# A new slot rule for VectorE, and a rearranged end, in a fused attention and MLP kernel

## The chip, the cores and the metric

One core of one Trainium2 chip. The time is device microseconds of one execution, the median of several runs on the same chip; the runs of one kernel lie within about half a microsecond of each other, in the first round up to 1.1 us. Profile spans are about 1.8 us shorter than times; positions count from a span's start.

## The reference, cut to what matters

```python
xn = layernorm(x)                                  # x: 2048 x 512, bfloat16
q = xn @ wq        # 32 heads of 16;  k, v = xn @ wk, xn @ wv: one head, shared
p = softmax(q k^T / 4);  o = p @ v                 # 2048 x 2048 scores for each head
s = o @ wo
g = silu(silu(xn @ w1) @ w2)                       # 512 -> 1792 -> 512
out = x + s * g
```

## The kernel before

The kernel holds its own scheduler. While the program is built, a planner places work on five engines with estimated durations and emits the instructions in that order; nothing is decided on the chip. Changed rules or seeds therefore give another fixed order.

Scores come as 2048 tiles of 128 keys by 512 queries: 32 groups of 64. A tile's exponential is made in one of two ways. **ScalarE** reads one to three tiles from PSUM, and each gives TensorE one PV product. **VectorE** makes an integer from the score with one multiply-add, whose bits read as bfloat16 approximate the exponential; GpSimd adds three constants to the bits of four such tiles at once (three "shifts"), and the tile gives four weighted PV products. A VectorE tile thus spares ScalarE 0.43 us and costs TensorE three more products. Seven PSUM banks hold scores and other products; the eighth collects PV.

The rule that decides how many of the 3 or 4 free banks of a score phase go to VectorE:

```python
bl = dve_backlog(); ab = act_need() - t
...
else:                                               # 3 or 4 banks are free
    want = 2 if n == 4 or ab > a_low else 1         # a_low: 1000 ns, varied at random
    ...
want = min(want, 2 if bl < two else 1 if bl < one else 0)
```

A group takes no new VectorE batch when few of its tiles are left:

```python
while g < NG and nleft[g] < (MARGIN if g < NG - 1 else MARGIN_END):   # 16, and 28 in the last group
    g += 1
```

The end. When the last PV product is placed, `last_norm` normalises on VectorE, each step for both column halves before the next step; then come four row tiles of the output product, four evictions, sums and stores:

```python
for h in range(2): t1.append(... transpose(f_sb[:, k, cols], bank(OB)[:, cols]))
for h in range(2): t2.append(... reciprocal ...)           # waits for t1[1]
for h in range(2): t3.append(... multiply ...)             # waits for t2[1]
for h in range(2): last_on.append(... transpose ...)       # waits for t3[1]
...
# per row tile r: four products o = 0..3 into bank r, those with o < 3 first
stt[r] = pl.add(scaled(tt, r))      # VectorE: fin = bank * 0.25 * tmp (tmp: this row tile's g)
# r < 3: TensorE adds x to fin by identity products, ScalarE copies it out; r = 3: VectorE adds x
...
if st["assigned"] == NG * SLOTS and st["expn"] == len(units) and not tail["made"]:
    make_tail()
```

The softmax here doesn't subtract the row's maximum and nothing guards it: scores larger than these inputs give would overflow.

## Time and profile before

| | before |
|---|---|
| time, median | 672.18 us |
| span of the profile | 670.4 us |
| TensorE / ScalarE / VectorE / GpSimd busy | 98 / 97 / 91 / 85% |
| last exponential on ScalarE ends | 661.5 us |
| last shift on GpSimd ends | 659.0 us |
| last PV product starts | 661.6 us |
| last copy of the output ends | 667.95 us |

A line of the groups or the timeline reads: start and duration (timeline), line, engine, operation, what is written from what is read, shapes and count; in brackets the idle time before it and what ended it. In a timeline line, a count merges instructions of one kind that follow each other. Line numbers belong to each kernel; L1228 before is L1282 after (PV), L860 is L866 (scores), L1157 is L1202 (shifts on GpSimd). The lines themselves are shown in the prediction.

Waits of TensorE are not read from its busy share here but worked out: score phases and runs of column-tiled products have fixed lengths when nothing holds them (the prediction derives them), and what the start-to-start times exceed these by is called "TensorE's waits" below.

### The profile page before, as it was taken

The page shows a single profiled execution, that of the slowest core. Times are in us where ns is not written, and L with a number is a line of the kernel's source. Part 1 is how long each engine was busy: PE and PEld are TensorE (multiplying, and loading weights), DVE is VectorE, ACT ScalarE, POOL GpSimd, SP SyncE. Part 2 cuts the span into 40 slices and gives each one's busy share as a digit, 9 for nine tenths or more (in the row PEclk, how much of TensorE's full clock was granted, in tenths as well). Part 3 has the DMA queues.
Part 4 walks back from the last instruction along what each step waited for, and adds up shares of the span by engine and source line. Part 5 has one row for each costly group of instructions (what it writes and reads, how often), then busy time and mean ns, then how long its engine had stood idle before and what let it go on. Part 6 is the DMA issues. An engine that isn't in the chain of part 4 may idle for free.

```text
span 670.4 us, 21190 instructions
## 1 busy us (share of the span) xinstructions
PE 658.4 (98%) x8958; PEld 191.4 (29%) x8958; DVE 608.6 (91%) x1085; ACT 651.5 (97%) x756; POOL 566.7 (85%) x564
## 2 busy tenths in 40 slices
PE   7999999999999999999999999999999999999997
PEld 4422222222222222222222222222222222222223
DVE  8989999999999999999899999998979999999963
ACT  6999999999999999999999999999999999999995
POOL 3049899998998889989899988898989998889993
PEclk9999999999999999999999999999999999999999
DMA  9500000000000000000000010000000000100000
GB/s 299 165 9 2 2 2 2 2 3 2 2 1 18 18 18 17 2 2 2 2 2 2 2 33 18 18 2 1 2 2 2 2 2 17 34 18 2 2 2 32
DMA packets 11821, 12.86 MB, mean 19 GB/s; under 512 B 1808, under 2 KB 11216, under 8 KB 11728
## 3 DMA queue, kind: packets, MB, share of 16 engines
q1 hardware_dynamic: 10928, 10.78, 5.0%
q8 instruction: 72, 1.18, 0.7%
q10 hardware_dynamic: 800, 0.72, 0.3%
q14 instruction: 21, 0.17, 0.1%
HBM read 8.95 MB, written 2.10 MB: 16 GB/s over the span
## 4 chain that ended last, share of the span: by engine, by line
PE 78%; ACT 12%; DVE 8%; issue 1%; DMA 0%; ACTq 0%; DVEq 0%
PE ps L1228 34%; PE ps L860 26%; PE ps L505 18%; ACT pa_sb L1572 11%; DVE db_sb L1090 3%; DVE stats_sb L452 1%; ACT t_sb L652 1%; DVE u_sb L654 1%; DMA ds_sb<-in_A_x_dram 0%; DVE xnT_sb L532 0%; DVE xn_sb L481 0%; DVE fin_sb L712 0%; DVE f_sb L1275 0%; DVE mv_sb L456 0%; DVE kt_sb L561 0%
## 5 line engine op out<-in xcount | busy, mean ns | idle before, releaser
L1157 POOL INT64_ADD ds_sb<-db_sb x552 | 561.0, 1038 | 87.5 <-DVE db_sb L1090 33.2
L1572 ACT ACTIVATE pa_sb<-ps 128x1024 bf16<-128x1024 f32 (+2 forms) x667 | 619.0, 1040 | 6.4 <-PE ps L860 3.5
L1090 DVE TENSOR_SCALAR db_sb<-ps 128x512 uint16<-128x512 f32 x736 | 474.4, 682 | 38.8 <-PE ps L860 27.5
L1228 PE MATMUL ps<-ds_sb,v_sb 128*32 128x512 bf16 x2208 | 265.9, 383 | 0.0
L860 PE MATMUL ps<-qt_sb,kt_sb 32*128 32x512 bf16 x2048 | 251.8, 385 | 4.4 <-ACT pa_sb L1572 1.1
L1228 PE MATMUL ps<-pa_sb,v_sb 128*32 128x512 bf16 x1312 | 242.4, 383 | 0.0
L1228 PE MATMUL ps<-db_sb,v_sb 128*32 128x512 bf16 x736 | 165.0, 384 | 0.3 <-DVE f_sb L1275 0.3
L860 PEld LDWEIGHTS ps<-qt_sb,kt_sb 32*128 32x128 bf16 x2048 | 63.1, 91 | 277.6 <-ACT pa_sb L1572 149.8
L1228 PEld LDWEIGHTS ps<-ds_sb,v_sb 128*32 128x32 bf16 x2208 | 65.6, 95 | 62.8 <-issue 46.1
L505 PE MATMUL ps<-xnT_sb,w_sb 128*32 128x512 bf16 x896 | 73.2, 384 | 0.0
L1228 PEld LDWEIGHTS ps<-pa_sb,v_sb 128*32 128x32 bf16 x1312 | 59.6, 95 | 36.5 <-issue 24.9
L505 PE MATMUL ps<-w_sb,u_sb 128*32 128x512 bf16 x816 | 64.2, 384 | 0.0
L1228 PEld LDWEIGHTS ps<-db_sb,v_sb 128*32 128x32 bf16 x736 | 40.9, 95 | 21.5 <-issue 14.5
L652 ACT ACTIVATE t_sb<-ps 128x512 bf16<-128x512 f32 x72 | 45.1, 627 | 0.0
L654 DVE SCALAR_TENSOR_TENSOR u_sb<-t_sb,ps 128x512 bf16<-128x512 bf16 x56 | 38.3, 683 | 1.3 <-ACT t_sb L652 0.3
L694 PE MATMUL ps<-w_sb,u_sb 32*128 32x512 bf16 x80 | 30.8, 385 | 0.0
L505 PEld LDWEIGHTS ps<-xnT_sb,w_sb 128*32 128x32 bf16 x896 | 17.5, 94 | 26.6 <-issue 20.6
L654 DVE SCALAR_TENSOR_TENSOR tmp_sb<-t_sb,ps 128x512 bf16<-128x512 bf16 x16 | 11.0, 688 | 12.3 <-ACT t_sb L652 12.2
L505 PEld LDWEIGHTS ps<-w_sb,u_sb 128*32 128x32 bf16 x816 | 15.6, 95 | 22.3 <-issue 18.5
L1275 DVE STREAM_TRANSPOSE f_sb<-ps 128x512 f32<-128x512 f32 x31 | 21.9, 707 | 0.1
L505 PE MATMUL ps<-wo_sb,on_sb 128*32 128x512 bf16 x256 | 19.2, 383 | 0.0
L505 PE MATMUL ps<-xnT_sb,wq_sb 128*32 128x512 bf16 x240 | 18.9, 384 | 0.0
(71 smaller groups left out, 161.9 us busy)
## 6 DMA issues: line engine op xcount, KB each, us to landing
w_sb<-in_B_w_dram SPq DMA_DIRECT2D x2, 1792.0 KB, 13.4
xr_sb<-in_A_x_dram SPq DMA_DIRECT2D x16, 128.0 KB, 2.3
out_dram<-ob_sb SPq DMA_DIRECT2D x16, 128.0 KB, 1.7
ds_sb<-in_A_x_dram SPq DMA_DIRECT2D x3, 512.0 KB, 6.9
wq_sb<-in_A_wq_dram SPq DMA_DIRECT2D x1, 512.0 KB, 5.1
wo_sb<-in_A_wo_dram SPq DMA_DIRECT2D x1, 512.0 KB, 16.0
kt_sb<-kt_sb ACTq DMA_DIRECT2D x4, 112.0 KB, 4.2
ds_sb<-in_A_x_dram ACTq DMA_DIRECT2D x2, 128.0 KB, 2.9
```

Of the source, the lines that this page charges most:

```text
L452: ts_ = pl.add(Task(DV, 593.0, lambda v, t=t: v.bn_stats(stats_sb[:, t, :], x_tile(t)), [xkey(t)], [("st", t)], 1 + j, gate=(lambda j=j: S ...
L505: last = h.matmul(bank(b)[32 * j:32 * (j + 1), 0:n], lhsT=lhs(j), rhs=rhs, start=start, stop=stop, tile_position=(0, 32 * j), skip_group_c ...
L652: t1 = Task(AC, 490.0, lambda a: a.activation(t_sb[:, k, :], src, ACT.Tanh, scale=scale), [held], [("t", k)], 0, [t0])
L654: t2 = Task(DV, T_P, lambda v: v.scalar_tensor_tensor(out=dst, in0=t_sb[:, k, :], scalar=1.0, in1=src, op0=ALU.add, op1=ALU.mult), [held, ...
L694: return (lambda pe: pe.matmul(bank(b), lhsT=u_sb[rows, ft, r * P:(r + 1) * P], rhs=w2_sb[rows, ft, :], start=False, stop=last, tile_posit ...
L860: return pe.matmul(bank(b), lhsT=kt_sb[32 * i:32 * i + 32, g % 2, kt * P:(kt + 1) * P], rhs=qt_sb[32 * i:32 * i + 32, (g // 2) % NQR, :], ...
L1090: bt.P[i] = pl.add(Task(DV, T_P, lambda v, b=b, i=i, bb=bt.b: v.tensor_scalar(db_sb[:, bb, i * NQ:(i + 1) * NQ], bank(b), 128.0 * LOG2E, 1 ...
L1157: whole["po"].append(pl.add(Task(PO, T_P64, lambda g, cols=cols: g.int64_add(ds_sb[:, s, cols].bitcast(U64), db_sb[:, bt.b, cols].bitcast( ...
L1228: h = pe.matmul(bank(OB)[32 * i:32 * (i + 1), :], lhsT=lhs, rhs=rhs, start=s0, stop=s1, tile_position=(0, 32 * i), skip_group_check=True)
L1275: t1 = pl.add(Task(DV, T_TR, lambda v: v.transpose(f_sb[:, k, :], bank(OB)), [("ps", OB)], [("F", k)], 1, [norm.get(("m", g - 2))]))
L1572: op = pl.place(AC, 0.8333 * NQ * n + T_AF, lambda a: a.activation(pa_sb[:, s * NQ:(s + n) * NQ].rearrange("p (b n) -> p b n", n=NQ), ps3[ ...
```

## The change

It keeps the amount of work and moves its order. The slot rule looks at the PV queue: with three free banks VectorE gets two when fewer than about ten PV entries are queued, else one. (For four free banks the new code also has a branch that gives one instead of two.) Ten seeds with a spread of 0.3 replace eight with 0.1. In the last group VectorE may start batches until 20 tiles are left, and may make shifts itself. ScalarE's last tiles (up to six) are done in two query halves, so that the first half is normalised while the second is still being computed. Two of the four last evictions go through ScalarE, the tail's banks are taken in the order in which they come free, and the tail is made as soon as the MLP is finished, before the last exponentials.

```diff
-SEEDS, STRETCH, SPREAD = (1020, 3123, 1104, 3421, 7220, 2660, 1802, 97), 64, 0.1
+SEEDS, STRETCH, SPREAD = (2502, 4652, 1398, 4134, 3319, 6151, 8548, 1413, 942, 5642), 64, 0.3
-MARGIN, MARGIN_END = 16, 28
+MARGIN, MARGIN_END = 16, 20
+Q3, Q4, J3, J4, N3, N4, SOLO = 10, -1, 1, 2, 1, 2, 0          # and QUEUE = 10
+END_DV = 40
+RH, EVR, SC_PRIO, MT_EARLY = 6, (0, 2), 0, 1
 ...
-                want = 2 if n == 4 or ab > a_low else 1
+                queue = sum(len(q) for g in range(st["gO"], min(st["gO"] + 2, NG)) for q in pvq[g])
+                held = any(not a.fixed for a in active)
+                if held:
+                    want = J4 + (queue < vary(Q4)) if n == 4 else J3 + (queue < vary(Q3))
+                else:
+                    want = N4 if n == 4 else max(N3, 2 * (queue < vary(QUEUE)))
+                if ab > a_low:
+                    want = 2
 ...
-                on_place=placed_dv, ports=2, gate=lambda: URG_SPLIT and urgent() or len(shifts) >= DV_MIN))
+                on_place=placed_dv, ports=2, gate=lambda: len(shifts) >= DV_MIN or bt.g == NG - 1 and nleft[bt.g] < END_DV))
 ...
+            if r in EVR:       # in scaled(): ScalarE takes the row tile out of PSUM, VectorE multiplies in SBUF
+                ev = pl.add(Task(AC, 490.0, lambda a: a.activation(xn_sb[:, r, :], bank(b), ACT.Copy, scale=0.25), ...
 ...
-            if st["assigned"] == NG * SLOTS and st["expn"] == len(units) and not tail["made"]:
+            if st["assigned"] == NG * SLOTS and (MT_EARLY and not active and st["job"] == len(jobs) or st["expn"] == len(units)) and not tail["made"] and all(
+                    tt in tmp_task for tt in range(NT - 4, NT)):
 ...
+        def begin_halves():    # the last <= RH tiles of ScalarE, each exponential for columns 0:256, then 256:512
 ...                             # last_norm(g, h) then runs for each half when its own PV products are placed
```

Other new code (wider pieces, a meter for jobs, late or single tiles) is off at these settings: PIECE_MIN of 9 is over the length of the jobs it now names, METER is empty, LATE and SOLO are 0.

## The prediction

> **What bounds the kernel now.** I read the page first (busy shares, the chain), then the groups by form, then TensorE's timeline in mid-kernel, then the waits, and last the timelines of the final 25 us. First the page's first lines and the by-engine line of the chain that ended last:
>
> ```profile
> span 670.4 us, 21190 instructions
> PE 658.4 (98%) x8958; PEld 191.4 (29%) x8958; DVE 608.6 (91%) x1085; ACT 651.5 (97%) x756; POOL 566.7 (85%) x564
> ...
> PE 78%; ACT 12%; DVE 8%; issue 1%; DMA 0%; ACTq 0%; DVEq 0%
> ```
>
> TensorE and ScalarE both look full, but "busy" for TensorE is modelled, so it alone decides nothing. TensorE's own timeline at 302 us shows the structure:
>
> ```profile
> 302.18 0.39 PE L860 MATMUL ps<-qt_sb,kt_sb 32*128 32x512 bf16 x3
> 302.51 0.40 PE L1228 MATMUL ps<-pa_sb,v_sb 128*32 128x512 bf16 x3
> ...
> 303.27 0.39 PE L860 MATMUL ps<-qt_sb,kt_sb 32*128 32x512 bf16 x4
> ...
> 304.14 0.39 PE L860 MATMUL ps<-qt_sb,kt_sb 32*128 32x512 bf16 x3
> ```
>
> Score products (row-tiled, 3 or 4 side by side) alternate with runs of column-tiled products: PV, projections, MLP. Going by starts: a score phase takes 0.32 us (302.18 to 302.51), whether it holds 3 or 4 products; the 12-product run after it 0.76 (302.51 to 303.27); an 8-product run 0.54. So a run costs about 0.216 per four products plus 0.114 for the switch, a score phase 0.321. The kernel before issues 642 score phases and 639 such runs with 1634 rounds of four: 642 x 0.321 + 639 x 0.114 + 1634 x 0.216 = 631.9 us. From the first run to the last the same pieces take 11.6 us more, summed start to start over the whole trace. That 11.6 is all that TensorE ever waits in them; it is spread evenly, 0.4 to 1.1 us per 50 us after the first 100.
>
> ScalarE, starts again: 667 exponentials, 1312 score tiles; a pair (128x1024) goes every 0.90 us, a single every 0.48, so 0.427 per tile plus 0.05 per instruction. With 72 tanh at 0.48: 594 + 34 = 628 us, first exponential at 11.5, last ended at 661.5. It has some 20 us of slack, part of it the prologue. So TensorE is the tighter one; ScalarE stops it for moments only, and they are seldom seen as waits:
>
> ```profile
> ACT pa_sb L1572 <- PE ps L860: 3.5, 10, 1.1
> ```
>
> That is the longest of ScalarE's waits for the exponentials (us in total, times, longest). Last the end: VectorE, then ScalarE, from 646 us on:
>
> ```profile
> 646.61 1.37 DVE L1090 TENSOR_SCALAR db_sb<-ps 128x512 uint16<-128x512 f32 x2
> 650.29 0.69 DVE L654 SCALAR_TENSOR_TENSOR tmp_sb<-t_sb,ps 128x512 bf16<-128x512 bf16 x1 [2.30 <-ACT t_sb L652]
> 660.63 0.69 DVE L654 SCALAR_TENSOR_TENSOR tmp_sb<-t_sb,ps 128x512 bf16<-128x512 bf16 x1 [9.65 <-ACT t_sb L652]
> 662.00 0.78 DVE L1243 STREAM_TRANSPOSE f_sb<-ps 128x256 f32<-128x256 f32 x2 [0.69 <-PE ps L1228]
> 662.70 0.31 DVE L1247 RECIPROCAL rcp_sb<-f_sb 128x8 f32<-128x8 f32 x2
> 662.94 0.46 DVE L1251 TENSOR_TENSOR otr_sb<-f_sb,rcp_sb 128x128 bf16<-128x128 f32 x2
> 663.31 0.76 DVE L1258 STREAM_TRANSPOSE on_sb<-otr_sb 128x256 bf16<-128x256 bf16 x2
> 664.26 2.61 DVE L712 SCALAR_TENSOR_TENSOR fin_sb<-ps,tmp_sb 128x512 bf16<-128x512 f32 x4 [0.18 <-PE ps L505]
> ```
>
> ```profile
> 660.37 1.14 ACT L1572 ACTIVATE pa_sb<-ps 128x1024 bf16<-128x1024 f32 x1
> 665.86 0.60 ACT L1440 ACTIVATE ob_sb<-ps 128x512 bf16<-128x512 f32 x1 [4.35 <-PE ps L1435]
> 666.75 1.20 ACT L1440 ACTIVATE ob_sb<-ps 128x512 bf16<-128x512 f32 x2 [0.30 <-PE ps L1435]
> ```
>
> VectorE makes its last score tile at 647.3 and then is idle for two long stretches, while ScalarE does the rest alone. After the last exponential (661.51) nothing overlaps: PV, both halves of the normalisation on VectorE (2.07 us), four evictions on VectorE (2.61), a sum, a copy, a store. From the last PV product (661.56) to the end of the last copy (667.95) is 6.39 us, and 2.4 more to the end of the span.
>
> **What the Trainium skill says.** "Perfetto Trace Analysis", section Identifying the Most-Contended Engine, says that matmul occupancy is no good measure of how near TensorE is to its limit, because pipelined instructions look smaller. Here it misleads the other way as well (busy hides the switches), so I use start-to-start times. The same page, section Optimizing Scalar/DVE Operations, gives ScalarE on PSUM some 51 ns of overhead per instruction; the trace agrees (0.904 for 1024 columns against 0.477 for 512 leaves 0.05). It also says that where an engine causes bubbles elsewhere, breaking up instructions may let work complete sooner: that is the idea of the halves. "VectorE: DVE Perf Modes", section The perf-mode tier table, lists tensor_scalar in bf16 within SBUF as 4x, 693 ns at 2048 elements; the shifts now also given to VectorE are of this kind (16 bits). No run so far shows one: VectorE has none in the kernel before. GpSimd takes 1.01 us, start to start, for each of its own. "DMA: Bandwidth & Descriptors" has about 2.0 us of fixed cost per transfer; the last store here takes 1.7, and neither kernel can shorten it.
>
> **The change part by part.** I counted instructions in the order in which both builds issue them; no time comes from there.
>
> Total work. Score tiles stay 2048 and VectorE's share stays 736 exactly; so do the 2208 shifted and 736 unshifted PV products. ScalarE keeps 1312 tiles, in 677 instead of 667 instructions (pairs 637 to 624, singles 26 to 41, triples 4 to 6, and 6 half-width ones): +10 x 0.05 = +0.5 us on ScalarE, which has slack. TensorE: score phases 642 to 640, column-tiled runs 639 to 638, rounds 1634 in both: 631.1 against 631.9, so -0.8 us.
>
> The PV-queue rule and the new seeds and spread. They change only who takes which tile and in which order. The rule gives VectorE two of three tiles when the PV queue is short, which turns pairs into singles; the counts (+15 singles) say that it fires rarely. It can only recover part of TensorE's 11.6 us. About 4 us of them lie before 100 us, where the prologue is the cause, so some 7 are in reach. The order was evidently searched again over ten stretches instead of eight; I allow -2.2 us, three tenths of what is in reach, and this is the softest term.
>
> The end margin (28 to 20) and shifts on VectorE (8 of them, GpSimd 552 to 544). VectorE works where it idled 10 us, but its total is unchanged, so it does eight tiles fewer elsewhere. Since TensorE is full in both places, I count 0 for itself. The eight shifts cost about 8 x 0.6 = 5 us of VectorE time (estimate from the skill's figure), inside that idle stretch, and keep GpSimd's queue (back to back from 646.79 to 658.98) from becoming the end when VectorE passes its last tile later.
>
> The halves. The order shows five tiles, not six, in halves: six exponentials in place of three, +3 x 0.05 on ScalarE. The first half's normalisation now runs while ScalarE computes the second half. After the last PV there is one chain: transpose 0.43, reciprocal 0.18, multiply 0.27, transpose 0.42 = 1.30, with waits between perhaps 1.45, instead of 2.07: -0.6.
>
> The evictions. Of the four serial ones (2.61), two go to ScalarE (0.60 each, parallel) and leave a 0.41 multiply, 0.33 start to start, on VectorE. VectorE then has 0.6 + 0.33 + 0.6 + 0.33 + a 0.33 add = 2.2 to its end instead of 2.94, and its first one need not wait for TensorE: the first half's products are done by then. Last copy, counted from the last PV start: 0.4 to the transpose, 1.45, products and evacuation up to 2.9, multiply 3.75, sum 4.2, copy 4.8; before 6.39: -1.6 for halves and evictions together. Against it, 36 output products instead of 52 are left after the last PV, so 16 (four rounds, 0.86 us) move ahead of it. As TensorE is full there, +0.9. Bank choice by release removes waits of at most tenths; counted in these sums.
>
> Sum: -0.8 + 0.9 - 1.6 - 2.2 = -3.7. 672.1 - 3.7 = 668.4 us.
>
> **The rivals.** (1) The search finds nothing and only the end counts: -1.5, so 670.6. For it: TensorE already waits only 1.8% of its time, evenly. (2) The rule really feeds TensorE and most of the reachable 7 us goes: 663 to 665. For it: ScalarE has 20 us of slack, so bubbles come from order alone; against it: counts hardly move. (3) The end is given back: eight later VectorE tiles each bring four PV products that depend on shifts; if they land after the last exponential, or a shift holds the port against GpSimd, TensorE sits idle at about 660 and the time is 671 to 673. The 8 shifts on VectorE speak against it.
>
> **Range and chances.** Between rivals 1 and 2: 665.6 to 670.6 should hold it 8 times in 10. Faster by 2% needs under 658.7: more than all waits of TensorE plus the tail's gain could give; 0.02. Slower by 2% needs +13 us: 0.01. Within 2%: 0.97.
>
> **What would show it.** Right: last PV to last copy about 4.8 us; TensorE's waits, start to start, 9 to 10 us; 8 VectorE shifts of about 0.7 us between the last VectorE score tiles and the last normalisation; ScalarE evacuations beside VectorE's. Wrong: waits unchanged or larger, an idle gap of TensorE before the last PV, or a tail that still takes 6 us.

## The result, and the profile after

The changed kernel takes 669.78 us (669.76 to 669.82, 4 runs), the kernel before 672.18 us beside it: a ratio of 0.9964, interval 0.9947 to 0.9981, so 2.4 us. By the 2% measure it is the same time. It lies in the range predicted, 1.4 us above the value.

The page's span, busy shares, and the chain by engine, after:

```profile
span 668.0 us, 21223 instructions
PE 658.0 (99%) x8962; PEld 191.2 (29%) x8963; DVE 615.0 (92%) x1093; ACT 652.1 (98%) x768; POOL 558.7 (84%) x556
...
PE 74%; ACT 17%; DVE 7%; issue 1%; DMA 0%; POOL 0%; ACTq 0%; DVEq 0%
```

The busy times hardly differ (TensorE 658.4 to 658.0 us). The chain by engine has lost some TensorE and gained ScalarE, but these are shares of the whole span and say nothing of the end: asked for the stretch from 640 us on alone, the chain of either kernel holds no exponential of ScalarE. VectorE's last stretch:

```profile
645.60 3.10 DVE L1196 TENSOR_SCALAR ds_sb<-db_sb 128x2048 uint16<-128x2048 uint16 x5
...
654.35 1.29 DVE L1002 TENSOR_SCALAR db_sb<-ps 128x512 uint16<-128x512 f32 x2 [0.61 <-PE ps L866]
655.67 1.90 DVE L1196 TENSOR_SCALAR ds_sb<-db_sb 128x2048 uint16<-128x2048 uint16 x3
659.28 0.45 DVE L1306 STREAM_TRANSPOSE f_sb<-ps 128x256 f32<-128x256 f32 x1 [1.71 <-PE ps L1282]
...
660.69 0.41 DVE L1306 STREAM_TRANSPOSE f_sb<-ps 128x256 f32<-128x256 f32 x1
...
662.10 0.69 DVE L719 SCALAR_TENSOR_TENSOR fin_sb<-ps,tmp_sb 128x512 bf16<-128x512 f32 x1
...
664.07 0.42 DVE L731 TENSOR_TENSOR ob_sb<-fin_sb,xr_sb 128x512 bf16<-128x512 bf16 x1
```

VectorE makes score tiles until 655.6 us instead of 648.0, and eight shifts at 0.60 us start to start, five of them before its last score tiles and three after. While it made the five, GpSimd stood idle, and went on when they were done (whether for a buffer, or because a shift held the port as the prediction's third rival feared, the trace does not say):

```profile
648.79 1.04 POOL L1202 INT64_ADD ds_sb<-db_sb  x1 [3.60 <-DVE ds_sb L1196]
```

The first half's transpose starts at 659.28, before the last exponential ends. From there VectorE works to 664.49 with hardly a gap, and the chain that ended last runs through it (view --critical: start, us, what):

```profile
659.18 0.07 PE ps L1282
659.25 0.02 issue
659.28 0.46 DVE f_sb L1306
...
660.77 0.34 DVE f_sb L1306
...
662.14 0.65 DVE fin_sb L719
```

So in the changed kernel it is PV of the first half on TensorE, then both normalisations and the evictions on VectorE, that set the end. ScalarE's last stretch:

```profile
657.52 2.64 ACT L1667 ACTIVATE pa_sb<-ps 128x512 bf16<-128x512 f32 x6
661.88 0.60 ACT L714 ACTIVATE xn_sb<-ps 128x512 bf16<-128x512 f32 x1 [1.73 <-PE ps L511]
...
663.72 1.57 ACT L1508 ACTIVATE ob_sb<-ps 128x512 bf16<-128x512 f32 x3 [0.36 <-PE ps L1503]
```

The six half-width exponentials end at 660.16 (1.35 us earlier than the last one before); the last PV product starts at 660.28 (1.29 earlier); the last copy ends at 665.30 instead of 667.95. From last PV to last copy it is 5.02 us instead of 6.38. Of those 2.65 us, 0.3 are lost behind them: from the last copy to the end of the span it takes 2.72 us instead of 2.46. The four stores, before and after, are

```profile
666.48 2.07 SPq L718 DMA_DIRECT2D out_dram<-ob_sb  x4
664.35 1.81 SPq L725 DMA_DIRECT2D out_dram<-ob_sb  x4
```

SyncE issues them one after the other. In the changed kernel the issues follow each other after 0.39, 0.48 and 0.50 us, so the last one comes 0.41 us after the last copy, not 0.14; from issue to landing it takes 1.85 us, as before (1.86). That is the 0.3.

TensorE's waits fall from 11.6 to 9.8 us. But the scores do not come earlier for it: the 1984th score product (the end of the last group but one) starts at 636.5 us before and at 636.3 after. What TensorE has gained by then is in other work. At 636.4 us, 112 MLP products of the second layer (two row tiles) were still to be issued before, and 56 (one row tile) after; VectorE evicts the last row tile's result (its `tmp`) at 660.6 us before, at 651.1 after. Against the 56 stand 12 PV products that are done later (4060 by then instead of 4072). The net 44 are eleven rounds of four, 2.4 us at the prediction's 0.216: about what the smaller waits and the fewer phases make together.

### The profile page after: what moved, and what is told of

The parts are those of the page before. It is cut to its first block, busy times and chain, and to the rows that moved or that the text cites. A ratio compares the mean times of both kernels' runs of the same rounds, so it can differ in the third digit from the quotient of the medians. Undisturbed runs are those within 1.5% of the kernel's fastest.

```text
span 668.0 us, 21223 instructions
## 1 busy us (share of the span) xinstructions
PE 658.0 (99%) x8962; PEld 191.2 (29%) x8963; DVE 615.0 (92%) x1093; ACT 652.1 (98%) x768; POOL 558.7 (84%) x556
## 4 chain that ended last, share of the span: by engine, by line
PE 74%; ACT 17%; DVE 7%; issue 1%; DMA 0%; POOL 0%; ACTq 0%; DVEq 0%
PE ps L1282 32%; PE ps L866 25%; PE ps L511 16%; ACT pa_sb L1717 16%; DVE db_sb L1002 2%; ACT t_sb L669 1%; DVE stats_sb L458 1%; DVE u_sb L671 1%; DVE xnT_sb L538 0%; DMA ds_sb<-in_A_x_dram 0%; DVE xn_sb L487 0%; POOL ds_sb L1202 0%; DVE fin_sb L719 0%; DVE f_sb L1338 0%; DVE mv_sb L462 0%
## 5 line engine op out<-in xcount | busy, mean ns | idle before, releaser
L1202 POOL INT64_ADD ds_sb<-db_sb x544 | 553.1, 1038 | 91.6 <-DVE db_sb L1002 34.9
L1282 PE MATMUL ps<-ds_sb,v_sb 128*32 128x512 bf16 x2208 | 274.4, 383 | 0.0
L1282 PE MATMUL ps<-pa_sb,v_sb 128*32 128x512 bf16 x1317 | 245.8, 382 | 0.0
L1282 PE MATMUL ps<-db_sb,v_sb 128*32 128x512 bf16 x736 | 176.2, 383 | 0.0
L1282 PEld LDWEIGHTS ps<-ds_sb,v_sb 128*32 128x32 bf16 x2208 | 68.4, 95 | 60.4 <-issue 41.9
L1282 PEld LDWEIGHTS ps<-db_sb,v_sb 128*32 128x32 bf16 x736 | 43.7, 95 | 20.3 <-issue 15.6
L618 PE MATMUL ps<-w_sb,u_sb 32*128 32x512 bf16 x76 | 29.2, 384 | 0.0
L1342 DVE TENSOR_TENSOR otr_sb<-f_sb,rcp_sb 128x256 bf16<-128x256 f32 x31 | 12.9, 417 | 1.4 <-POOL ds_sb L1202 1.1
```

The lines of the kernel that those rows point to most:

```text
L618: return (lambda pe: pe.matmul(bank(b), lhsT=lhs(k, rows, 0, P), rhs=rhs(k, rows), start=False, stop=last, tile_position=(32 * i, 0), skip ...
L1202: whole["po"].append(pl.add(Task(PO, T_P64, lambda g, cols=cols: g.int64_add(ds_sb[:, s, cols].bitcast(U64), db_sb[:, bt.b, cols].bitcast( ...
L1282: h = pe.matmul(bank(OB)[32 * i:32 * (i + 1), cols], lhsT=lhs, rhs=rhs, start=s0, stop=s1, tile_position=(0, 32 * i), skip_group_check=True)
L1342: t3 = pl.add(Task(DV, 332.0, lambda v: v.tensor_tensor(o3[:, :, val:val + DH], f3[:, :, val:val + DH], rcp_sb[:, k, :].unsqueeze(2).to_br ...
```

## The experiments

All twelve are versions of the changed kernel, all gave correct results. This table has what their traces show (us); the median of the kernel before beside each was 672.12 to 672.18.

| run | TensorE's waits | last MLP result evicted | last exponential ends | last GpSimd shift ends | last PV starts | last PV to last copy | time |
|---|---|---|---|---|---|---|---|
| before | 11.6 | 660.6 | 661.5 | 659.0 | 661.6 | 6.38 | 672.1 |
| after | 9.8 | 651.1 | 660.2 | 655.1 | 660.3 | 5.02 | 669.8 |
| end alone | 11.9 | 663.0 | 659.5 | 660.5 | 662.3 | 6.56 | 673.3 |
| order alone | 10.8 | 652.3 | 659.7 | 659.3 | 659.7 | 6.71 | 670.8 |
| old rule, new seeds | 12.5 | 663.7 | 659.7 | 661.1 | 662.3 | 6.96 | 673.7 |
| new rule, old seeds | 9.9 | 649.1 | 660.6 | 654.9 | 661.1 | 5.18 | 670.9 |
| new rule, no random numbers | 11.0 | 650.5 | 661.5 | 661.6 | 663.0 | 5.15 | 672.6 |
| old rule, no random numbers | 11.6 | 662.2 | 660.3 | 656.6 | 661.4 | 6.55 | 672.3 |

### The end alone, and the order alone

Edit for the end alone: old rule and old seeds in the changed kernel (with a guard that the tail is made only when all banks are accounted for, since the build failed without it). TensorE's order is that of the kernel before up to its last 85 rows of merged instructions.

```diff
-SEEDS, STRETCH, SPREAD = (2502, ..., 5642), 64, 0.3
+SEEDS, STRETCH, SPREAD = (1020, ..., 97), 64, 0.1
-                (the new rule)
+                want = 2 if n == 4 or ab > a_low else 1
```

> The end's parts alone (halves, evacuations on ScalarE, tail banks, shifts on VectorE, margin 20) with the slot rule and the seeds of the kernel before: TensorE's order is that of the kernel before up to its last 85 rows. Theory A (the order in the middle brought most of it, since the shorter chain after the last PV is paid for by output products that move ahead of it): 671.5 to 672.2 us. Theory B (the end brought its 1.4 us in full and the middle the rest): 670.6 to 671.0 us.

Edit for the order alone, in which TensorE's order is that of the changed kernel up to its last 84 rows:

```diff
-MARGIN_END = 20;  END_DV = 40;  RH, EVR, SC_PRIO, MT_EARLY = 6, (0, 2), 0, 1
+MARGIN_END = 28;  END_DV = 0;   RH, EVR, SC_PRIO, MT_EARLY = 0, (), 0, 0
```

> The slot rule and the seeds alone, the end as in the kernel before: TensorE's order is that of the changed kernel up to its last 84 rows. Theory A: 669.8 to 670.4 us. Theory B: 670.9 to 671.4 us. If the parts add, the savings of this run and of the run with the end alone sum to 2.4 us within 0.4.

Measured: the end alone 673.28 us, ratio 1.0017 (1.0003 to 1.0031), slower than before; the order alone 670.78, ratio 0.9980. Both theories fall in their common assumption that the parts add: -1.1 (slower) and +1.4 us of savings make 0.2, and together they save 2.4. The end costs 1.1 us on the old order and gains 1.0 on the new one. The trace of the end alone says why (TensorE, then ScalarE, then GpSimd):

```profile
661.54 0.83 PE L618 MATMUL ps<-w_sb,u_sb 32*128 32x512 bf16 x2
662.30 0.29 PE L1277 MATMUL ps<-pa_sb,v_sb 128*32 128x256 bf16 x2
662.31 3.73 PE L511 MATMUL ps<-wo_sb,on_sb 128*32 128x512 bf16 x64
```

```profile
658.03 1.42 ACT L1662 ACTIVATE pa_sb<-ps 128x256 bf16<-128x256 f32 x4
662.41 0.60 ACT L669 ACTIVATE t_sb<-ps 128x512 bf16<-128x512 f32 x1 [2.95 <-PE ps L618]
```

```profile
647.33 13.20 POOL L1197 INT64_ADD ds_sb<-db_sb  x13 [2.91 <-DVE ds_sb L1191]
```

ScalarE is done with its exponentials at 659.45, two microseconds before the kernel before, and then waits 2.95 us for TensorE. TensorE is still on PV and on the last MLP row tile (L618 is a piece of it); GpSimd, with thirteen shifts in a row to 660.53, is close behind. The tail may only be made when the MLP is finished, so all 64 output products stand after the last PV, where the changed kernel has 33. In this order TensorE bounds the end. Relieving ScalarE gains nothing, and the four VectorE tiles more that this build has (740 instead of 736) cost TensorE twelve products, some 0.65 us at 0.216 per four.

In the order alone the last PV even starts 0.54 us earlier than in the changed kernel, but the old tail takes 6.71 us after it, 60 output products among them. Against it the changed end is 1.7 us shorter after the last PV and starts 0.54 later: the two terms that the prediction set at -1.6 and +0.9.

### Rule and seeds

The edits are the two halves of the diff of the end alone, each by itself (the old rule also has the guard on the tail); all of the changed end stays.

> The changed kernel with the old rule for VectorE's slots and the new seeds and spread. If the rule is what cuts TensorE's waits (start to start) from 11.6 to 9.8 us, they go back to 11 to 12 us and the time to 671.3 to 672. If the new seeds do it, waits stay at 9.5 to 10.3 us and the time at 669.6 to 670.4.

> The changed kernel with the new rule but the seeds, stretch count and spread of the kernel before. If the rule brings it: 669.6 to 670.4 us, waits below 10.3 us. If the search over seeds brings it: 671 to 672 us, waits 11 us or more.

Measured: old rule with new seeds 673.72 us, ratio 1.0027 (1.0014 to 1.0039); new rule with old seeds 670.87, ratio 0.9981. So the theory of the rule fits better, though both times lie outside what it stated: taking the rule away costs 3.9 us, not 2, and the seeds still bring 1.1. The waits went the way of the rule's theory (12.5, above the 11 to 12 stated, and 9.9). But some of the 3.9 us is the draw: the build with the old rule has two stalls of TensorE, 0.62 us at 408.7 and 0.47 us at 427.7, where the changed kernel has none over 0.15 us between 100 and 650 us. Two draws prove little, so I took a third, without random numbers (both builds also have the guard; built again, the new-rule program is the same without it, as the changed kernel is with it):

```diff
-SEEDS, STRETCH, SPREAD = (2502, ..., 5642), 64, 0.3
+SEEDS, STRETCH, SPREAD = (), 64, 0.0
```

> The changed kernel with no random numbers in its scheduler at all, new slot rule: a third draw of the order. If the rule itself (VectorE gets two of three tiles when fewer than ten PV entries are queued) is what lets TensorE run ahead with the MLP products, 56 of them (one product of the last four) are left at the end of the last-but-one group, as in the changed kernel, and the time is 669.5 to 671.5 us. If the order is luck, it may fall anywhere from 669 to 674.

> The same without random numbers, old slot rule, all the rest of the end as changed. Rule theory: two MLP products (112) are left as in the kernel before, the last tanh comes after the last exponential, and the time is 672.5 to 674.5 us, at least 2 us over the run with the new rule. Luck theory: within 1.5 us of that run, either way.

Measured: 672.60 us with the new rule, 672.28 with the old (the edges of their intervals, 0.9994 and 1.0024, 0.9986 and 1.0019, overlap). The rule as such is therefore not worth 2 us: over three draws it is -2.4, -3.9 and +0.3. Of the first expectation the count of MLP products held and the time did not; the times of the two fit the second expectation's theory of luck. In all three draws the new rule has the last MLP result out by 649 to 652 us, the old one at 662 to 664; and with the old rule, the time from last PV to last copy is 6.5 to 7.0, with the new one 5.0 to 5.2. (All three builds with the old rule have 740 VectorE tiles, those with the new one 736; I did not separate this.)

What takes the gain away in the third draw is in part that it was never there: by 636.4 us the build with the new rule is 56 MLP products ahead of the one with the old rule, but 44 PV products and six score products behind it (in the two other draws at most four and two behind), and TensorE has stalled for 0.56 us at 429.3. At the end GpSimd adds to it:

```profile
651.46 10.16 POOL L1202 INT64_ADD ds_sb<-db_sb  x10 [1.12 <-PE ps L1282]
```

These ten shifts end at 661.62; VectorE made only two in this order. The two halves share a PSUM bank, so the second half's PV may start only when the first half, shifted products and all, has been transposed out of it: the last PV starts at 663.04, 1.6 us after the last exponential.

How can a rule about VectorE's slots make the MLP finish earlier? The kernels, built again with the planner's decisions printed, say that it hardly acts. In the changed kernel it wants another number of tiles than the old rule in 7 of 640 score phases, all before 38 us; in six of them VectorE takes no tile under either rule, so a single decision changes: at 37.2 us of the planner's time VectorE gets two of three tiles and not one. The branch for four banks never changes anything. The builds without random numbers prove it: with that one decision forced, the old rule gives the program of the new rule, instruction for instruction. The traces agree. In each of the three pairs ScalarE's instructions are the same up to the 48th, at 38.4 to 38.6 us, which is a single tile with the new rule and a pair with the old. So the experiments compare two courses of the planner that part at one tile (with seeds the new rule also draws more random numbers, which is a second difference), not feeding by a short PV queue against none; and the three draws are not independent, since ScalarE's order with the new rule is the same in all three up to 273 us. Why the one course has the MLP done earlier stays open.

### The parts of the end, one at a time

On the changed order the parts of the end can be undone singly; the order stays the same up to the last rows.

Without the halves:

```diff
-RH, EVR, SC_PRIO, MT_EARLY = 6, (0, 2), 0, 1
+RH, EVR, SC_PRIO, MT_EARLY = 0, (0, 2), 0, 1
```

> The changed kernel without the two query halves; all else and TensorE's order up to its last ten rows stay. If the halves take the first normalisation out of the last chain as the prediction says (2.07 us on VectorE back in place of 1.41), +0.5 to +1.0 us: 670.3 to 670.8. If VectorE's evictions bound the end whatever the halves, within 0.2 of 669.8.

670.44 us (ratio 0.9975 to before): the halves are worth 0.7 us, inside the first expectation. From last PV to last copy it is 6.09 instead of 5.02, and the last PV starts 0.3 earlier, as fewer output products stand ahead of it (40 after it instead of 33).

All evictions on VectorE:

```diff
-RH, EVR, SC_PRIO, MT_EARLY = 6, (0, 2), 0, 1
+RH, EVR, SC_PRIO, MT_EARLY = 6, (), 0, 1
```

> The changed kernel with all four last evictions on VectorE. VectorE is busy without a gap from 659.3 to 664.5 us in the changed kernel, so two multiplies from PSUM (0.60 each) in place of two from SBUF (0.33) should cost 0.4 to 0.6 us: 670.2 to 670.4. If TensorE's sums or the stores bound the end, within 0.15 of 669.8.

670.01 us (ratio 0.9968): worth 0.2, between the two expectations, and less than VectorE's own saving. VectorE's four evictions take 2.44 us in one run; the last copy ends 0.2 us later after the last PV (5.21 instead of 5.02).

No shifts on VectorE:

```diff
-END_DV = 40
+END_DV = 0
```

> The changed kernel without shifts on VectorE, so eight more on GpSimd. If GpSimd's shifts become the end (the prediction's third rival), GpSimd runs without gaps to about 659 to 661 us, the last PV waits for it and the time is 670.5 to 672. If PV has enough other work, within 0.3 of 669.8.

670.46 us (ratio 0.9974): worth 0.7. Here is GpSimd:

```profile
647.31 12.19 POOL L1202 INT64_ADD ds_sb<-db_sb  x12 [1.00 <-DVE otr_sb L1342]
```

It runs without a gap to 659.50, as long as before the change (658.98), and the last PV starts at 661.02 instead of 660.28, 0.9 us after the last exponential. The theory that GpSimd becomes the end fits, though the time lies just under what it stated (670.5).

The old end margin:

```diff
-MARGIN, MARGIN_END = 16, 20
+MARGIN, MARGIN_END = 16, 28
```

> The changed kernel with the old end margin of 28, so VectorE's last score tiles come earlier. The prediction counted 0 for the margin by itself: within 0.3 of 669.8. If it matters that ScalarE works alone for longer at the end, the last exponential ends about 1 us later and the time is 670.5 to 671.2.

671.60 us (ratio 0.9991, interval 0.9976 to 1.0006): it costs 1.8 us, more than any other part of the end, and more than either theory stated. ScalarE and TensorE in this run:

```profile
659.29 2.86 ACT L1667 ACTIVATE pa_sb<-ps 128x512 bf16<-128x512 f32 x6
```

```profile
657.80 0.40 PE L1282 MATMUL ps<-pa_sb,v_sb 128*32 128x512 bf16 x3
657.82 0.59 PE L511 MATMUL ps<-zer_sb 128*32 128x256 bf16 x8
658.71 0.39 PE L1282 MATMUL ps<-pa_sb,v_sb 128*32 128x512 bf16 x2 [0.30 <-ACT pa_sb L1717]
658.72 0.60 PE L511 MATMUL ps<-zer_sb 128*32 128x256 bf16 x8
```

The margin here decides one batch: VectorE gets 732 tiles and not 736, and ScalarE has 52 to do after 636.4 us instead of 48. Its last exponential ends at 662.15, 2.0 us later (four tiles at 0.43 are 1.7). TensorE has so little left that the planner fills it with products of zeros (zer_sb), and it waits for ScalarE. The chain that ended last says the same of this run:

```profile
651.20 7.47 ACT pa_sb L1717 x10
658.67 0.04 issue
658.71 0.29 PE ps L1282
```

So with four tiles more on ScalarE the end is bound by ScalarE. In the changed kernel it is not: its chain has no exponential there, and TensorE has no gap over 0.1 us from 640 to 662 us. Nor is it the margin as such that costs: the order alone has the margin of 28 too, but 736 VectorE tiles, and its last exponential ends at 659.7 (its chain, too, runs through ScalarE, so ScalarE is near to the bound in this order).

### Two attempts at a better version

An end margin of 8 carries on in the same direction (this build and the next also have the guard on the tail):

```diff
-MARGIN, MARGIN_END = 16, 20
+MARGIN, MARGIN_END = 16, 8
```

> The changed kernel with an end margin of 8: VectorE takes still more of the last group's tiles. If ScalarE's lone stretch still bounds the end, the last exponential ends 0.8 to 1.7 us earlier and the time is 668.2 to 669.2. If PV that waits for shifts has become the bound, as with no shifts on VectorE, the last PV comes later than 660.3 us and the time is 670 to 671.5.

672.54 us (ratio 1.0007): the second expectation, and beyond it. ScalarE is done at 658.23, 1.9 us earlier, but

```profile
655.70 6.26 POOL L1202 INT64_ADD ds_sb<-db_sb  x6 [0.61 <-DVE db_sb L1002]
```

This build has 740 VectorE tiles. GpSimd's last shift ends at 661.96 and the last PV starts at 663.09. A margin of 20 stands between the two bounds; margins between 8 and 20 were not run.

Output products of the first half issued as soon as they can be, and three evictions through ScalarE:

```diff
-RH, EVR, SC_PRIO, MT_EARLY = 6, (0, 2), 0, 1
+RH, EVR, SC_PRIO, MT_EARLY = 6, (0, 1, 2), 0, 1
-            for n, (_, r, o, emit) in enumerate(tail["items"][:1]):
+            (first any o = 3 whose o < 3 are issued and whose half is normalised; else the first item)
```

> An attempt at a better version: in the changed kernel the output products of the first query half are issued as soon as that half is normalised, not after all 48 others, and all three evictions but the last go to ScalarE. VectorE, busy without a gap from 659.3 to 664.5 us in the changed kernel, loses 0.27 us and is no longer waited for by the second sum: 669.2 to 669.6 us. If the stores bound the end: 669.7 to 669.9.

669.55 us (669.44 to 669.59, 4 runs; ratio 0.9962, interval 0.9947 to 0.9977), inside the first expectation but only 0.2 us below the changed kernel's median in another round, with overlapping intervals: not clearly a gain. The evacuations begin 0.7 us earlier (661.16 instead of 661.88), but TensorE's last sum waits for VectorE, whose last multiply was placed behind the add for the fourth row tile:

```profile
664.44 0.39 PE L1506 MATMUL ps<-fin_sb,ident 128*128 128x512 bf16 x1 [0.40 <-DVE fin_sb L716]
```

So the last copy ends no earlier (665.46). The span still ends 0.3 us earlier, 2.29 us after the last copy instead of 2.72: the first store is issued 0.28 us earlier (664.07), and the last only 0.03 us after its copy.

## Why the prediction was right or wrong

**Right, and in its terms:** the work is equal and TensorE's fixed pieces save 0.8 us. The waits fall by 1.8 us where 2.2 were allowed, and what TensorE won went into MLP products (net 44 products, 2.4 us). From last PV to last copy it took 5.0 us where 4.8 were worked out. The eight shifts take 0.60 us each from start to start. The prediction had that figure without a derivation (the 693 ns it cites would make 5.5 us of eight, not 5), and five of the eight came before VectorE's last score tiles, not after. Five tiles in halves. The advice that the prediction cites for breaking up instructions (the Trainium skill, "Perfetto Trace Analysis", section Optimizing Scalar/DVE Operations) is given for a ScalarE that is not saturated; here it is 97% busy over the span, but waits 1.73 us after its last exponential, and undoing the halves costs 0.7 us.

**Mis-sized: the store.** The prediction took the 2.4 us after the last copy as fixed. They became 2.7, because SyncE's issues of the four stores queue up (the last is issued 0.41 us after its copy, not 0.14). That is 0.3 of the 1.4 us by which the prediction was too low. (The last store itself takes 1.86 and 1.85 us from issue to landing; the prediction's 1.7 is the median of all sixteen.)

**Mis-sized: the sum before the last PV.** -0.8 - 2.2 + 0.9 makes -2.1; measured is -1.3. The waits account for 0.4 of the 0.8 missing. Three output products more than counted stand ahead of the last PV (33 are left after it, not 36), 0.16 us by the prediction's own rate; the rest the runs do not split further. With the store's 0.3 and 0.2 of the tail itself (-1.4 instead of -1.6) that is the whole error.

**The margin: right for the change, wrong as a rule.** "Since TensorE is full in both places, I count 0 for itself" rests on the premise that VectorE's total is unchanged. In the change as a whole the premise holds (736 tiles, TensorE without a gap), so the 0 does not spoil the sum. By itself the margin moves whole batches: 28 in the changed kernel leaves ScalarE four tiles more and costs 1.8 us, 8 gives VectorE four more and costs 2.8.

**Wrong: the sum of independent terms.** On the old order the end costs 1.1 us, on the new one it gains 1.0. The first rival ("only the end counts: -1.5") failed for the same reason: the end pays only behind an order in which the MLP is finished first. That the sum still came close is in part luck.

**Wrong in what it credits: the rule and the seeds.** The prediction allowed 2.2 us for a rule that feeds TensorE when the PV queue is short and for a wider search. "It fires rarely" was right: it decides once. But one tile moved at 37 us gives another order from there on, and the order alone is worth 1.4 us. With either set of seeds the new course is worth as much as the whole change or more, without random numbers nothing. The size of the term came out, its reason did not.

**The third rival** (the end is given back when late VectorE tiles wait for shifts) did not occur in the changed kernel, but it did in three of the runs (no VectorE shifts, no random numbers with the new rule, margin 8): last shift at 659.5 to 662.0 us, last PV 0.9 to 4.9 us after the last exponential. That the eight VectorE shifts speak against it is confirmed by the run without them.

Open: why the course that the rule opens brings the MLP forward, and whether another draw of seeds would do as well with the old rule.

## What to carry to other kernels

An end is a race of several engines, and a change that relieves one is worth what the next one allows: undo the parts singly on the new order, and also put them on the old one. Where several bounds (ScalarE's tiles, GpSimd's shifts, TensorE's leftover products) lie within a few microseconds of each other, a threshold such as the margin can have its best value in the middle, as here, where four tiles either way cost 1.8 and 2.8 us. A scheduler that draws its order needs more than one draw before a rule is credited with the gain; and print how often the rule decides, for here it was once in 640 phases.

## What the Trainium skill lacked or had wrong

- "TensorEngine Tiling (Array Packing)", section Key Properties, says that changing the tiling mode drains TensorE, but gives no size. Here a score phase takes 0.321 us start to start and a column-tiled run 0.216 us per four products plus 0.114, so about 0.11 us per switch (an estimate: the score phase is taken as one round of 0.216 and a switch), some 1280 times in a kernel of 670 us: about a fifth of its time.
- "Perfetto Trace Analysis", section Identifying the Most-Contended Engine, says that matmul busy time is no measure of distance to the roofline; it lacks that busy time does not show waits either. TensorE's busy time moved from 658.4 to 658.0 us, while its waits, start to start, fell from 11.6 to 9.8.
- "VectorE: DVE Perf Modes", section The perf-mode tier table, has 693 ns for this kind of tensor_scalar at 2048 elements; the profile has 687, so it agrees. The table has no figure for such instructions back to back; here they follow each other every 0.60 us (five in 3.10). The page's section on the TRN2 errata has a formula that gives 594 ns, which it calls too low for one instruction; it is close to this spacing.
- No page has a time for GpSimd's 64-bit integer add, which does the same shift: 1.04 us in the profile, 1.01 us start to start.
